# Attention emitted in two halves a pair, inside an attention and two-MoE kernel on one core

## The chip, the cores and the metric

The kernel runs on one NeuronCore of a Trainium2 chip. The metric is the device time of one execution in microseconds, the median of three runs, lower is better. PE is the matrix engine (TensorE), DVE the vector engine, ACT the scalar engine, POOL is GpSimd, and SP issues most DMAs.

## The reference

Three stages follow one another over 4 x 768 = 3072 tokens. Banded attention with sink columns (8 heads of 64, window 128, 4 sinks) gives x; a product of two projections and two more matrices gives x again; a router sends every token to one of 8 experts.

```
keep = is_sink | in_window                       # pos < 4, or 0 <= query - key < 128
scores = where(keep, (q @ k.T) / sqrt(64), -1e9)
a = exp(scores - max);  a = a / (sum(a) + 1e-9)
x = a @ v                                        # then heads side by side: [3072, 512]
x = ((x @ w1) * (x @ w2)) @ w3 @ w_out           # first MoE block, w1 and w2 [512, 1024]
e = argmax(x @ w_gate + modality_bias[modality_id])
out = gate * relu(x @ w1[e]) @ w2[e]             # second MoE block, 8 experts
```

## The kernel before

**Tiles.** The tokens are cut in 12 units of 256 (three to a batch entry, `c` = 0, 1, 2), and the heads in 4 pairs of two. One step through attention is a pair `n` (unit `n // 4`, heads `n % 4`), 48 in all. A unit has two blocks of 128 queries, `j` = 0 and 1. The parts of a pair are these.

- `a_tqk(n)` makes q and k ready with their low parts (by PE for the first 8 pairs, by a transpose on DVE after that).
- `a_scores(n, j)`: 6 matmuls on L458 (three pairs, each for two heads in the two halves of 64 rows of the array) into the one buffer `sp`, then a masking copy (L475) and a maximum (L484) on DVE, two exponentials on ACT (L486), and, deferred, the normalization of `P` on DVE (`norm`, L491 to L497).
- `a_pt(n)` transposes `P` with 4 matmuls (L527); ACT copies the result to `ptf` (L531), and POOL makes two masked copies `ptp` (L536). `a_skT(n)` transposes the sink columns (L509).
- `a_pv(n)` is the product of P and v: 12 matmul instructions on L555 (8 where `c` is 0) with an output of 64 columns of the array for each head, and one for the sinks (L558). ACT and DVE then write the result into `xb` (L561, L566).

**First MoE block.** Units go through `moe1_stream` in 6 groups of two. A group `gr` is a row of pieces, each with a cost: 16 pieces "ab" (12 matmuls on L724, cost 2600), 8 pieces "x2" (6 matmuls on L712, cost 1300), and 8 pieces "late" (6 matmuls on L712, cost 1300) for its second unit. The cost `t` reaches 52,000 with the last "x2" and 62,400 with the last "late". Before the first "late" piece can write, ACT must empty the two `x2p` buffers of the first unit (`route_rows`, L772).

**What sets the order.** `att_stream` is a generator; each `yield` ends a step, and a pair `n` has 5 steps. After every MoE piece `front` calls `att_upto`, which runs attention steps up to a number that grows with `t`: 20 steps evenly over the first 52,000 (so step k of the group follows the first piece whose `t` is over 2600 (k - 1)), then 20 steps over the 8 "late" pieces. A group starts with four steps of its first pair already made. Pairs 9 to 47 lie in the groups 0 to 4; the last group has no attention. Deferred jobs run at the second `tick` after them, and both steps and pieces tick. The framework then puts out each engine's instructions in the order of emission, except that one which its plan finds not ready lets later ones go first. Engines work through their lists in order.

Before the change, the steps of a pair from the second on are: scores of block 0; transposes of pair n - 1; `a_tqk(n + 1)`; scores of block 1; product of pair n - 1.

Of the kernel before, what the change touches and what calls it, by code (L numbers as in the profile page):

```python
# [27 lines left out]
def attention_moe_moe_kernel(ctx, tc, q, k, v, w1, w2, w3, w_out, mod_id, w_gate, mod_bias, e_w1, e_w2, out,  # L28
# [57 lines left out]
    def tick():  # L86
        for fn in waiting[0]:
            fn()
        waiting[0], waiting[1] = waiting[1], []

    def settle():
        while waiting[0] or waiting[1]:
# [253 lines left out]
    def a_load(n):  # L346
        u, p = divmod(n, NP)
        b, c = divmod(u, NC)
        hs = slice(2 * p, 2 * p + 2)
        qk = att.tile([128, 2, UNIT], F32, tag="qk", bufs=2, name="qk")  # L350
        for x, src in enumerate((q, k)):
            if n < BY_PE:
                for j in range(2):
                    s0 = c * UNIT + j * 128
                    nc.sync.dma_start(out=qk[:, x, j * 128:(j + 1) * 128].rearrange("p (h d) -> p h d", h=2),
                                      in_=src[b, hs, s0:s0 + 128, :].rearrange("h s d -> s h d"))
                continue
            for g in range(4):
                h, d0 = 2 * p + g // 2, g % 2 * 32
                nc.sync.dma_start(out=qk[g * 32:(g + 1) * 32, x].rearrange("p (b i) -> p b i", i=32),  # L360
                                  in_=src[b, h, c * UNIT:(c + 1) * UNIT, d0:d0 + 32].rearrange("(b s) i -> s b i", s=32))
        nat[n] = qk

    def a_load_v(n):
        u, p = divmod(n, NP)
        b, c = divmod(u, NC)
        hs = slice(2 * p, 2 * p + 2)
        vn = att.tile([128, 3, 2, D], F32, tag="vn", bufs=3, name="vn")
        for j in range(0 if c else 1, 3):
            s0 = c * UNIT + (j - 1) * 128  # L370
            nc.sync.dma_start(out=vn[:, j], in_=v[b, hs, s0:s0 + 128, :].rearrange("h s d -> s h d"))
        stt["v", n] = vn
        if n and c == 0 and p == 0:
            a_load_sinks(b)
# [143 lines left out]
    def a_pt(n):  # L518
        u, p = divmod(n, NP)
        b, c = divmod(u, NC)  # L520
        P = stt["p", n]
        for j in range(2):
            stt.pop(("norm", n, j))()
        tp = ps_t.tile([128, 4, 128], F32, tag="t", name="pt")
        for j in range(2):
            for h in range(2):
                nc.tensor.transpose(out=tp[:, 2 * j + h, :], in_=P[:, j, h * (KW + NS):h * (KW + NS) + 128], identity=idf)  # L527
        full = att.tile([128, 4, 128], F32, tag="ptf", bufs=1, name="ptf")
        parts = att.tile([128, 2, 2, 2, 128], F32, tag="ptp", bufs=1, name="ptp")
        i0 = 0 if c else 1  # L530
        nc.scalar.activation(out=full[:, 2 * i0:4], in_=tp[:, 2 * i0:4], func=ACTF.Copy)  # L531
        if i0:
            nc.scalar.activation(out=parts[:, 0, 0], in_=tp[:, 0:2], func=ACTF.Copy)
        for a, op in enumerate((ALU.is_ge, ALU.is_gt)):
            sign = 1 - 2 * a
            nc.gpsimd.affine_select(out=parts[:, a, i0:2].rearrange("p j h q -> p (j h) q"), in_=full[:, 2 * i0:4],  # L536
                                    pattern=[[0, 4 - 2 * i0], [sign, 128]], compare_op=op, fill=0.0, base=0,
                                    channel_multiplier=-sign)
        stt["pt", n] = parts
# [34 lines left out]
    def att_stream():  # L574
        a_tqk(0); yield
        a_load(1)
        a_load_sinks(0)
        a_vsink(0)
        yield
        for n in range(NN):  # L580
            if n + 2 < NN:
                a_load(n + 2)
            a_scores(n, 0); yield
            if n:
                a_load_v(n)
                a_pt(n - 1); a_skT(n - 1); yield
            if n + 1 < NN:
                a_tqk(n + 1)
            yield
            a_scores(n, 1); yield  # L590
            if n:
                a_pv(n - 1)
                att_done[0] = n
                if n % (NP * NC) == 0:
                    a_vsink(n // (NP * NC))
            yield
        a_pt(NN - 1); a_skT(NN - 1); yield
        a_pv(NN - 1)
        att_done[0] = NN
        yield  # L600
# [412 lines left out]

    def front():
        att_it = att_stream() if banded else att_stream_full()
        steps = [0]

        def step_att():
            if next(att_it, 0) == 0:
                return False  # L1020
            steps[0] += 1
            tick()
            return True

        def att_upto(target):
            while steps[0] < target and step_att():
                pass

        unit_steps = ATT_STEPS * NP
        begun = 10 if banded else 4  # L1030
        wab_n = W_EARLY
        t = 0.0
        f64_ahead(2)
        if banded:
            a_load(0)
            a_load_v(0)
        f64_ahead(4)
        for i, c in enumerate(startup_stream()):
            t += c
            tick()  # L1040
            if att_done[0] < 2 * NP:
                att_upto(min(0.75 * (i + 1), 8) + 38 * t / 46700)
        early = []
        for gr in range(NU // 2):
            while att_done[0] < (2 * gr + 2) * NP:
                step_att()
            settle()
            last = gr == NU // 2 - 1
            if last:
                for _ in att_it:  # L1050
                    pass
                att_ctx.close()
                pool = p2a.enter_context(tc.tile_pool(name="p2a", bufs=1, side="right", reuse_waits="tile"))
                mem = mem_of(pool, wp, pool, pool, pool, pool, (ps_t, ps_ab, ps_x2, 1))
                p2a_pool.append(pool)
                mem["w1"] = halves(lambda: pool.tile([128, 1024], F32R, tag="w1", bufs=KD, name="w1"), mem["w"])
                rows0 = pool.tile([128, SLOT // 128, ROW], F32, name="xrows")
                t_banks = [mem["pt"], lambda: ps_x.tile([128, 512], F32, tag="x", name="x")]

                def next_bank():  # L1060
                    t_banks.reverse()
                    return t_banks[0]()

                mem["pt"] = next_bank

                def next_early(first=0):
                    slots.append(Slot(SLOT, (NU - 2 if slots else NU - 4) * UNIT, mem))
                    slots[-1].decide(first)

                def first_early():  # L1070
                    next_early(3)
                    slots[0].gather(rows0)

                first_early()
                early = [(10000 + 2000 * i, lambda i=i: slots[0].w1_piece(i)) for i in range(KD)]
                early += [(47000 + 1500 * i, next_early) for i in range(N_EARLY - 1)]
                early += [(57200 + 1300 * i, lambda i=i: slots[0].transposes(i)) for i in range(KD)]
            t, routed, s0 = 0.0, 0, steps[0]
            s1 = begun + (2 * gr + 3) * unit_steps
            for kind, c in moe1_stream(gr):  # L1080
                t += c
                tick()
                while gr == 0 and wab_n < KF and wab_n < W_EARLY + t / 4000:
                    wab_pair(wab_n)
                    wab_n += 1
                    if wab_n == KF:
                        wgate_by_expert()
                        start_ctx.close()
                        sp_[0] = m1_ctx.enter_context(tc.tile_pool(name="m1", bufs=1, reuse_waits="tile"))
                        consts_late()  # L1090
                        load_wgate()
                if last:
                    while early and t >= early[0][0]:
                        early.pop(0)[1]()
                    due = min(t, 46000) / 1100
                else:
                    due = min(t, 46000) / 1100
                while routed < due and kind != "late":
                    routed += 1
                    route_step()  # L1100
                if kind != "late":
                    att_upto(min(s0 + (s1 - s0) * t / 52000, s1))
                else:
                    att_upto(s1 + unit_steps * (t - 52000) / 10400)
            for _, fn in early:
                fn()
        settle()
# [131 lines left out]
```

## Time and profile before

| | |
|---|---|
| runs | 975.64, 975.77, 976.39 us (median 975.77) |
| the profiled execution | 975.55 us, span 973.8 us |
| PE | 932.9 us busy, 96% of the span |
| DVE | 651.8 us busy, 67% |
| ACT | 440.5 us busy, 45% |
| POOL | 167.2 us busy, 17% |

Starts of matmuls are recorded, their ends are modelled and overlap the next start. So a price on PE is best read from the distance between the starts of two rows, and not from the busy time.

### The profile page before, as it was taken

To read this page: it belongs to the slowest core of one execution; us is meant where nothing else is said; L and a number is where in the kernel's file an instruction comes from. 1 tells how busy PE (TensorE), PEld (TensorE's weight loads), DVE (VectorE), ACT (ScalarE), POOL (GpSimd) and SP (SyncE) were. 2 spreads that over 40 slices of the span, in tenths; PEclk is the share of its full clock that TensorE was granted. 3 is DMA by queue.
4 is the path that set the end of the run, shared out by engine and by line. 5 is a ranking of instruction groups with operands and counts; after the bars stand their busy time and mean duration, and the time that the engine had idled before them with its cause. 6 is when DMAs were issued, how large, how long until landed. Compare 5 with 4: busy or idle time off the path is not lost. (4 is left out here: it accounts for less than half of the span.)

```text
span 973.8 us, 15418 instructions
## 1 busy us (share of the span) xinstructions
PE 932.9 (96%) x4840; PEld 709.7 (73%) x4840; DVE 651.8 (67%) x1953; ACT 440.5 (45%) x1218; POOL 167.2 (17%) x253
## 2 busy tenths in 40 slices
PE   4899999999999999999999999999999999999995
PEld 3567677767776777677767776887888888888883
DVE  7956996699659964896599649929934374333422
ACT  3687763454335433553365334314433443344433
POOL 1111121111112111211111112213021214111010
PEclk9999999999999999999999999999999999999998
DMA  8754754123212231236123200512446465443331
GB/s 258 237 149 122 210 121 127 34 53 71 51 23 48 61 56 20 52 71 44 23 53 67 56 9 9 178 40 87 139 164 129 153 69 191 132 149 120 109 134 41
DMA packets 168933, 94.02 MB, mean 97 GB/s; under 512 B 140231, under 2 KB 148679, under 8 KB 168720
## 3 DMA queue, kind: packets, MB, share of 16 engines
q1 hardware_dynamic: 164080, 80.13, 33.6%
q0 software_dynamic: 4768, 12.88, 4.1%
q8 instruction: 39, 0.64, 0.3%
q14 instruction: 46, 0.38, 0.2%
HBM read 80.14 MB, written 13.09 MB: 96 GB/s over the span
## 5 line engine op out<-in xcount | busy, mean ns | idle before, releaser
L724 PE MATMUL ab<-xb,wab 128*128 128x512 f32 x1152 | 288.7, 397 | 1.0 <-DVE g L734 1.0
L724 PEld LDWEIGHTS ab<-xb,wab 128*128 128x128 f32 x1152 | 209.7, 188 | 46.0 <-PE sp L458 1.1
L970 PE MATMUL x<-w 128*128 128x512 f32 x600 | 141.0, 392 | 0.0
L785 DVE CUSTOM_DVE_ANT_0 junk<-rows,wgb 128x512 bf16<-128x512 f32 x192 | 135.7, 707 | 2.0 <-ACT rows L772 0.9
L712 PE MATMUL x2p<-w3o,gh 128*128 128x512 f32 x384 | 128.9, 411 | 0.5 <-ACT gh L701 0.5
L970 PEld LDWEIGHTS x<-w 128*128 128x128 f32 x600 | 111.6, 188 | 23.1 <-DVE w L202 0.4
L536 POOL TENSOR_SCALAR_AFFINE_SELECT ptp<-ptf 128x512 f32<-128x512 f32 (+1 forms) x96 | 66.5, 716 | 308.0 <-ACT ptf L531 308.0
L701 ACT ACTIVATE gh<-g 128x256 fp32r<-128x256 f32 x96 | 39.9, 416 | 119.2 <-DVE g L731 98.6
L486 ACT ACTIVATE P<-sp,st 128x132 f32<-128x132 f32 (+1 forms) x192 | 69.2, 366 | 51.5 <-DVE st L484 45.8
L712 PEld LDWEIGHTS x2p<-w3o,gh 128*128 128x128 f32 x384 | 67.2, 188 | 18.0 <-ACT gh L701 2.9
L202 DVE TENSOR_TENSOR w<-wst,w 128x512 fp32r<-128x512 f32 x112 | 71.4, 685 | 10.5 <-ACT w L201 10.5
L937 DVE SCALAR_TENSOR_TENSOR w<-ab,w 128x512 fp32r<-128x512 f32 x48 | 33.1, 690 | 64.4 <-ACT w L936 64.2
L712 PE MATMUL x2p<-w3o,gl 128*128 128x512 f32 x192 | 76.0, 396 | 0.0
L933 PE MATMUL ab<-w,w 128*128 128x512 f32 x288 | 74.9, 395 | 0.0
L933 PE MATMUL ab<-w 128*128 128x512 f32 x288 | 73.6, 391 | 0.0
L201 ACT ACTIVATE w<-wst 128x512 fp32r<-128x512 f32 x112 | 63.4, 628 | 4.5 <-DMA wst<-in_moe_w_dram 4.5
L458 PE MATMUL sp<-ring,qh 64*128 64x264 f32 (+1 forms) x384 | 61.1, 329 | 3.2 <-ACT P L486 2.2
L458 PEld LDWEIGHTS sp<-ring,qh 64*128 64x128 f32 x384 | 37.0, 185 | 35.8 <-ACT P L486 15.5
L933 PEld LDWEIGHTS ab<-w,w 128*128 128x128 f32 x288 | 53.9, 188 | 12.4
L933 PEld LDWEIGHTS ab<-w 128*128 128x128 f32 x288 | 54.1, 188 | 12.1
L936 ACT ACTIVATE w<-ab 128x512 fp32r<-128x512 f32 x48 | 28.7, 597 | 71.8 <-PE ab L933 71.4
L974 POOL DMA_INDIRECT out_dram<-late,ti x25 | 25.2, 1009 | 203.9 <-ACT late L973 166.6
(201 smaller groups left out, 1392.9 us busy)
## 6 DMA issues: line engine op xcount, KB each, us to landing
wst<-in_moe_w_dram SPq DMA_DIRECT2D x56, 512.0 KB
f64st<-in_moe_w_dram SPq DMA_DIRECT2D x32, 512.0 KB
vn<-in_v_dram SPq DMA_DIRECT2D x128, 64.0 KB
xs<-rows SPq DMA_DIRECT2D x12, 513.0 KB
qk<-in_q_dram SPq DMA_DIRECT2D x160, 32.0 KB
qk<-in_k_dram SPq DMA_DIRECT2D x160, 32.0 KB
f64st<-in_moe_w_out_dram SPq DMA_DIRECT2D x8, 512.0 KB
wgb<-wgt SPq DMA_DIRECT2D x1, 2048.0 KB
```

The lines of the kernel that those rows point to most:

```text
L201: nc.scalar.activation(out=hi, in_=src, func=ACTF.Copy)
L202: lo_eng.tensor_tensor(out=lo, in0=src, in1=f32(hi), op=ALU.subtract)
L458: nc.tensor.matmul(out=sp[:, h, c0:c0 + nk].rearrange("p (a b) -> p a b", b=KW), lhsT=a[hp, j, :], rhs=kr[hp, b_, blocks, c0:c0 + KW], sta ...
L486: nc.scalar.activation(out=rows[:, h], in_=seen[:, h], func=ACTF.Exp, bias=st[:, 0, h:h + 1], accum_out=st[:, 1, h:h + 1])
L536: nc.gpsimd.affine_select(out=parts[:, a, i0:2].rearrange("p j h q -> p (j h) q"), in_=full[:, 2 * i0:4], pattern=[[0, 4 - 2 * i0], [sign, ...
L701: nc.scalar.activation(out=gh, in_=g, func=ACTF.Copy)
L712: nc.tensor.matmul(out=x2p[t], lhsT=a[:, sl], rhs=b_, start=(f == 0 and i == 0), stop=(f == KF - 1 and i == 2))
L724: nc.tensor.matmul(out=bank[nm].rearrange("p (u t) -> p u t", u=2), lhsT=a, rhs=b_, start=(kk == 0 and i == 0), stop=(kk == KD - 1 and i = ...
L785: nc.vector.tensor_tensor_reduce(out=junk, in0=rows[:, t, 0:DM], in1=wgb[0][:, e, :], scale=1.0, scalar=0.0, op0=ALU.mult, op1=ALU.add, ac ...
L933: nc.tensor.matmul(out=hp, lhsT=a[:, fs], rhs=b_, start=(kk == 0 and i == 0), stop=(kk == KD - 1 and i == 2))
L937: nc.vector.scalar_tensor_tensor(out=h[:, 1], in0=hp, scalar=0.0, in1=f32(h[:, 0]), op0=ALU.max, op1=ALU.subtract)
L970: nc.tensor.matmul(out=op, lhsT=a[:, ts], rhs=b_, start=(f == 0 and i == 0), stop=(f == KF - 1 and i == 2))
```

## The change

For pairs with `n > 2 * NP`, that is 9 to 47, the five steps become: (A) the loads, the scores of block 0 and the transposes of pair n - 1; (B) `a_tqk(n + 1)`; (C) the scores of block 1 and the product of pair n - 1; and two empty steps. Nothing is computed otherwise, and no instruction is added or removed. A helper `in_order` would tie PE instructions to their order of emission, but it is used only where `strict[0]` is true, and nothing sets it so.

```diff
         for n in range(NN):
             if n + 2 < NN:
                 a_load(n + 2)
+            if n > 2 * NP:
+                a_load_v(n)
+                a_scores(n, 0)
+                a_pt(n - 1); a_skT(n - 1); yield
+                if n + 1 < NN:
+                    a_tqk(n + 1)
+                yield
+                a_scores(n, 1)
+                a_pv(n - 1)
+                att_done[0] = n
+                if n % (NP * NC) == 0:
+                    a_vsink(n // (NP * NC))
+                yield
+                yield
+                yield
+                continue
             a_scores(n, 0); yield
...
+        strict = [False]
 
         def step_att():
-            if next(att_it, 0) == 0:
+            if (in_order(lambda: next(att_it, 0)) if strict[0] else next(att_it, 0)) == 0:
                 return False
...
-            for kind, c in moe1_stream(gr):
+            strict[0] = False
+            moe_it = moe1_stream(gr)
+            while True:
+                piece = in_order(lambda: next(moe_it, None)) if strict[0] else next(moe_it, None)
+                if piece is None:
+                    break
+                kind, c = piece
```

## Rows read from the trace of the kernel before

**Rows 1.** The page: busy time of the engines over the span.
```profile
PE 932.9 (96%) x4840; PEld 709.7 (73%) x4840; DVE 651.8 (67%) x1953; ACT 440.5 (45%) x1218; POOL 167.2 (17%) x253
```
**Rows 2.** Windows: length, busy us of each engine, granted clock, DMA share, GB/s.
```profile
265.00:289.00 24.00, 24.00 (x132) 18.65 (x131) 11.65 (x38) 9.01 (x26) 4.74 (x8) 1.00 0.13 24
289.00:313.00 24.00, 22.25 (x137) 14.87 (x137) 21.65 (x68) 13.36 (x45) 4.78 (x9) 1.00 0.25 44
```
**Rows 3.** Groups by line on PE, 122 to 610 us (busy, mean, idle before).
```profile
L724 PE MATMUL ab<-xb,wab 128*128 128x512 f32 x973 | 246.8, 398 | 1.0 <-DVE g L734 1.0
...
L458 PE MATMUL sp<-ring,qh 64*128 64x264 f32 (+1 forms) x312 | 48.4, 328 | 2.1 <-ACT P L486 1.8
L555 PE MATMUL xp<-ptp,vn 128*64 128x128 f32 (+1 forms) x432 | 47.3, 323 | 2.9 <-issue 1.7 <-POOL ring L435 0.6 <-POOL ptp L536 0.3
L527 PE MATMUL pt<-idf,P 128*128 128x128 f32 x160 | 27.5, 278 | 4.7 <-DVE P L497 3.3 <-DVE wk L814 1.4
```
**Rows 4.** Timeline of PE, 252.9 to 262 us: start, length, instructions merged.
```profile
253.22 0.39 PE L712 MATMUL x2p<-w3o,gl 128*128 128x512 f32 x1
253.54 0.40 PE L458 MATMUL sp<-ring,qh 64*128 64x264 f32 x2
...
254.10 3.02 PE L724 MATMUL ab<-xb,wab 128*128 128x512 f32 x12
257.05 1.09 PE L555 MATMUL xp<-ptp,vn 128*64 128x256 f32 x12
...
258.29 2.90 PE L724 MATMUL ab<-xb,wab 128*128 128x512 f32 x12
261.13 0.40 PE L458 MATMUL sp<-ring,qh 64*128 64x264 f32 x2
```
**Rows 5.** Timeline of PE at 414 us.
```profile
413.87 0.39 PE L458 MATMUL sp<-ring,qh 64*128 64x264 f32 x2 [0.29 <-ACT P L486]
...
414.44 1.09 PE L555 MATMUL xp<-ptp,vn 128*64 128x256 f32 x12
```
**Rows 6.** Timeline of PE, 263 to 270 us.
```profile
263.17 2.89 PE L724 MATMUL ab<-xb,wab 128*128 128x512 f32 x12
265.90 0.60 PE L527 MATMUL pt<-idf,P 128*128 128x128 f32 x4
...
266.47 3.01 PE L724 MATMUL ab<-xb,wab 128*128 128x512 f32 x12
269.32 0.62 PE L712 MATMUL x2p<-w3o,gh 128*128 128x512 f32 x2
```
**Rows 7.** Timeline of PE, 389 to 395 us.
```profile
389.48 0.40 PE L712 MATMUL x2p<-w3o,gl 128*128 128x512 f32 x1
389.80 0.65 PE L555 MATMUL xp<-ptp,vn 128*64 128x256 f32 x2
390.38 0.74 PE L712 MATMUL x2p<-w3o,gh 128*128 128x512 f32 x2
...
391.29 0.86 PE L555 MATMUL xp<-ptp,vn 128*64 128x256 f32 x8
392.08 0.73 PE L712 MATMUL x2p<-w3o,gh 128*128 128x512 f32 x2
...
392.98 0.43 PE L555 MATMUL xp<-ptp,vn 128*64 128x128 f32 x2
...
393.65 0.39 PE L458 MATMUL sp<-ring,qh 64*128 64x264 f32 x2
...
394.22 0.66 PE L527 MATMUL pt<-idf,P 128*128 128x128 f32 x4
```
**Rows 8.** Timeline of ACT over the same stretch.
```profile
389.21 0.60 ACT L772 ACTIVATE rows<-x2p 128x512 f32<-128x512 f32 x1 [0.47 <-PE x2p L712]
...
390.71 0.61 ACT L772 ACTIVATE rows<-x2p 128x512 f32<-128x512 f32 x1
```
**Rows 9.** Timeline of PE at 407 us.
```profile
406.76 1.09 PE L555 MATMUL xp<-ptp,vn 128*64 128x256 f32 x12 [0.64 <-issue]
```

More of the change, by code (lines that the diff above doesn't have):

```diff
@@ L89, in tick, with in_order @@
         waiting[0], waiting[1] = waiting[1], []
+    issued = [None]
+    def in_order(fn):
+        traced = nc.cur_bb.bb.instructions
+        first = len(traced)
+        got = fn()
+        for ins in traced[first:]:
+            if ins.engine == mybir.EngineType.PE:
+                if issued[0] is not None:
+                    tc.add_manual_dep(ins, issued[0], mybir.DependencyInfo(mybir.DependencyClass.NoSync,
+                                                                           mybir.DependencyReason.DATA), reason="in order")
+                issued[0] = ins.name
+        return got
     def settle():
```

## The prediction, as it was made

> **What bounds the kernel now.** I read the page first: PE is busy for 96% of the span and no other engine for more than 73%, the weight loads of PE itself included [rows 1]. So PE's list sets the time, and a change can win only by making what PE does cheaper or by taking away waits on it. The groups by line, over the stretch in which the changed pairs run, bound the second: before scores, product and transposes PE sat idle for 2.1 + 2.9 + 4.7 = 9.7 us in all [rows 3]. The windows say where. In a regular stretch of a group PE has no gap at all and DVE works for 11.65 of 24 us; in the stretch that starts with the "late" pieces DVE works for 21.65 of 24 us and PE has 1.75 us without work [rows 2]. So there are two kinds of place: a regular one, where PE alone decides and its order follows the emission, and a crowded one (some 45 us a group, from the late pieces to the first fifth of the next group), where attention runs as its results come in and MoE fills the holes. The clock is 1.00 of full speed, the 2.4 GHz level, in both [rows 2]. What is left is the price of PE's order, and the timeline has it.
>
> **Prices of a change of kind.** A row of MoE matmuls runs at 0.2275 us each: twelve take from 263.17 to 265.90, 2.73 us, and the transposes that follow cost no extra to enter [rows 6]. Into scores there is an entry price: 253.22 to 253.54 is 0.32, so 0.09 more than 0.23 [rows 4]. Twelve MoE matmuls between scores and a product take from 254.10 to 257.05, 2.95 us, 0.22 over 2.73: 0.09 is the entry to the product and 0.13 an exit price behind the scores. Twelve between a product and scores take 2.84 (258.29 to 261.13): entry 0.09, and behind a product next to no exit, 0.02 [rows 4]. Behind transposes twelve take 2.85 (266.47 to 269.32), so these have an exit of 0.12 of their own [rows 6].
>
> **The change, part by part.** No instruction is added or removed, and the order in which attention puts out its PE work stays the same (scores 0, transposes, scores 1, product). Only the MoE pieces between them move.
>
> *Scores of block 1 next to the product (C).* What stood on both sides of the MoE row, exit 0.13 and entry 0.09, goes, if scores then run into the product for no more than they run into MoE. Six scores matmuls to MoE take 0.56 (253.54 to 254.10) [rows 4]; the one case in which a product follows directly takes 0.57 (413.87 to 414.44) [rows 5]. So a C saves 0.22 - 0.01 = 0.21 us. How many: the steps C are the 4th, 9th, 14th and 19th of a group, and the product before was the 6th, 11th, 16th and 21st. The 4th falls in the crowded stretch, so I count three a group and four in the first group, which has little in front of it: 16 for five groups, 3.4 us. Both ends: all 39 pairs give 8.2 us, none 0. I take 16, since only in the regular stretch does the order on PE follow the emission.
>
> *Scores of block 0 next to the transposes (A).* The scores' exit of 0.13 goes. Scores to transposes takes 0.57 (393.65 to 394.22), against 0.56, and the four transposes behind them last 0.66 [rows 7] against 0.60 [rows 6]. So 0.13 - 0.01 - 0.06 = 0.06, times 16: 1.0 us. Ends: 0 and 39 x 0.06 = 2.3.
>
> *The junction to the late pieces.* The product that was step 21, first behind the first late piece, becomes part of step 19 and leaves this place. Here PE must wait for ACT to empty the two buffers (0.60 us each, at 389.21 and 390.71) [rows 8], and the product is what fills the hole, torn in three parts by MoE threes. From 389.80 to 393.65 are 3.85 us; without six MoE matmuls (1.37) and the entry of the scores (0.09) that is 2.39 [rows 7], against 1.24 for a whole product (257.05 to 258.29) [rows 4]: 1.15 lost. The five groups have such a place at 194.16, 290.31, 389.80, 487.28 and 583.44 us, three torn in three and two in two parts; for two I take half, so 3 x 1.15 + 2 x 0.58 = 4.6 us. What fills the hole now is A: transposes, which enter free, and scores, which may be cut up to twice at 0.22 each (entry and exit), 5 x 0.44 = 2.2. I take 4.6 - 2.2 = 2.4; ends 0 (something is torn as dearly) and 4.6.
>
> *What I cost at nothing.* The loads of v are put out one step sooner on SP's queue, behind the same loads of q and k; v(n) is read only a pair later, which covers it. The empty steps only let deferred jobs run. ACT and DVE get scores and transposes, or scores and product, in one bunch; in the regular stretch DVE's 12 free us of 24 [rows 2] cover that, and the banks that it must empty for MoE have the next x2 or ab piece (6 or 12 x 0.2275) in front of their next use. If that cover went, PE would stand before L724, which idled 1.0 us in all this stretch [rows 3]. Waits of PE in the crowded stretch I leave as they are; they can change by up to the 9.7 us that exist [rows 3], either way. `strict[0]` is never true, so the helper costs nothing.
>
> *Sum.* 3.4 + 1.0 + 2.4 = 6.8 us off the profiled execution of 975.55: 968.75. The median of the runs is 0.22 above that execution, so about 969.0.
>
> A rule that speaks against C: the Trainium skill, TensorE: Matmul & The Clock Gate, Part 3, says that a weight load runs under a matmul in flight only when the two use different row groups. Scores use halves of the rows and the product all, so by it the first weight load of a product (64 columns, 53 ns by the formula of that page's section on LDWEIGHTS, an estimate) would stand open in each C; 16 of these are 0.85 us and the sum would be 5.9. The row at 414.44 does not show it, so my sum leaves it out.
>
> **Rivals.**
> 1. *The junction stays as dear* (chance 0.15). The plan tears whatever stands there: a cut scores group, or the product of the step 19 pushed back to the hole. For it: the hole itself remains, since ACT's two copies remain [rows 8]. Against it: transposes are in reach and enter free. Time: 975.77 - 4.4 = 971.4.
> 2. *Next to each other is worth nothing* (0.15). The only uninterrupted case of C is a single row, and it stands behind a wait [rows 5]; if scores ran into the product 0.2 us later than into MoE, as they would if a weight load that the last MoE matmul hid stood open, or if the plan finds the product not ready and puts MoE between, C saves nothing. With the junction unchanged too, 975.77 - 1 = 974.8, down to no change.
> 3. *The product waits for POOL* (0.20; the other side). Between a pair's transposes and its product in the late stretch stand one MoE piece and the scores where there were two pieces and the scores: 6 x 0.2275 = 1.37 us less for ACT, POOL's two masked copies and DVE's low part of the sinks. One product there already waits 0.64 us [rows 9]. There are 4 such pairs a group, 20 in all. If all wait 0.64, that is 12.8 - 6.8 = 6.0 us slower, 981.8; it decides from 6.8 / 0.64 = 11 waits on, and 14 give 977.9. Behind the waiting product on PE's list is everything, MoE too. Against it: products that the plan finds late are passed by MoE matmuls, and in the crowded stretch the order of attention itself does not change.
>
> **How the numbers follow.** Forecast 0.50, with its own range 965.5 to 971.4 (the junction between 0 and 4.6, waits changed by 1 or 2 us); rivals 0.15, 0.15 and 0.20. A measurement of this kernel can tell 0.2%, about 1.95 us, from no change, so 973.8 and 977.7 are the bounds. Faster: 0.50 + 0.15 = 0.65; within: 0.15; slower: 0.20. To hold eight in ten the range takes the forecast and the first two rivals whole and the foot of the third: 965.5 to 977.
>
> **What would show it.** In the timeline of a regular stretch scores are followed within 0.57 us by a product or by transposes, and the twelve MoE matmuls behind take 2.73 to 2.85 us, not 2.95. Around the late pieces the product is in one part, 1.24 us. The idle time before L458, L555 and L527 stays near 9.7 us, and that before L724 near 1.0. The first late piece comes some 1.3 us a group earlier than before, added up group by group. Wrong would be: MoE matmuls between scores and product in the regular stretch (rival 2), torn scores at the junction with the same total (rival 1), or idle time before L555 of more than 7 us (rival 3).

## The result, and the profile after

The changed kernel takes 965.06 us (median of 964.83, 964.92, 965.20 and 965.63) against 975.87 for the kernel before, run on the same chip: a ratio of 0.9889, 95% interval 0.9872 to 0.9907, 10.8 us faster. The forecast was 969.0, 6.8 us faster. The sign was right, and each of the three places that the prediction named did gain; 4 us were missing, and the time lies 0.44 us below the range.

Line numbers move: L724 is now L755, L712 is L743, L458 is L473, L555 is L570, L527 is L542, L772 is L803. So do the copies and sums around them: DVE's normalization of `P`, L497, is L512, ACT's exponentials, L486, are L501, POOL's masked copies, L536, are L551, and DVE's subtraction that makes the low part of the sinks, L514, is L529.

The page of the kernel after, busy time by engine, answers to [rows 1]. PE has the same 4840 matmuls and is still busy for 96% of a span of 963.0 us.

```profile
PE 924.0 (96%) x4840; PEld 711.2 (74%) x4840; DVE 649.3 (67%) x1953; ACT 440.2 (46%) x1218; POOL 168.2 (17%) x253
```

The timeline of PE in a regular stretch of the kernel after (start, length, merged instructions; it answers to [rows 4, 5, 6]). Scores at 250.87 run into a product at 251.44, 0.57 us later, and scores at 259.59 into transposes at 260.16, 0.57 us later. Behind the product, six MoE matmuls take 252.68 to 254.06, 1.38 us, which is 6 at 0.2275 and next to nothing, and 24 more take 5.53, which is 24 at 0.2275 and 0.07 for the entry to scores: nothing is left of the exit price that stood behind scores.

```profile
250.87 0.39 PE L473 MATMUL sp<-ring,qh 64*128 64x264 f32 x2
...
251.44 1.09 PE L570 MATMUL xp<-ptp,vn 128*64 128x256 f32 x12
...
252.68 0.63 PE L743 MATMUL x2p<-w3o,gh 128*128 128x512 f32 x2
...
254.06 5.60 PE L755 MATMUL ab<-xb,wab 128*128 128x512 f32 x24
259.59 0.40 PE L473 MATMUL sp<-ring,qh 64*128 64x264 f32 x2
...
260.16 0.66 PE L542 MATMUL pt<-idf,P 128*128 128x128 f32 x4
```

The junction to the late pieces, PE of the kernel after (answers to [rows 7]). The product is whole, 285.36 to 286.60, 1.24 us. A single matmul of the next scores fills the hole in front of the first late piece (0.32 us, 289.41 to 289.73), then six MoE matmuls go in one row, and the other five scores follow. The scores are torn, as I had feared, once and not twice. But the one cut is dear: 0.32 us for the single matmul, and the six MoE matmuls behind it take 1.59 us to the next scores instead of 1.37, while the five scores that are left take 0.56, as long as six. That is 0.54 us.

```profile
284.79 0.39 PE L473 MATMUL sp<-ring,qh 64*128 64x264 f32 x2
...
285.36 1.09 PE L570 MATMUL xp<-ptp,vn 128*64 128x256 f32 x12
...
286.60 0.62 PE L743 MATMUL x2p<-w3o,gh 128*128 128x512 f32 x2
...
289.41 0.39 PE L473 MATMUL sp<-ring,qh 64*128 64x264 f32 x1
289.73 0.73 PE L743 MATMUL x2p<-w3o,gh 128*128 128x512 f32 x2
...
291.32 0.39 PE L473 MATMUL sp<-ring,qh 64*128 64x264 f32 x1
...
291.88 0.66 PE L542 MATMUL pt<-idf,P 128*128 128x128 f32 x4
```

ACT over the same stretch (answers to [rows 8]). The two copies that empty the buffers start 0.84 us apart, not 1.50, since no exponentials of the last scores lie between them any more.

```profile
288.84 0.60 ACT L803 ACTIVATE rows<-x2p 128x512 f32<-128x512 f32 x1 [0.43 <-PE x2p L743]
...
289.68 0.58 ACT L803 ACTIVATE rows<-x2p 128x512 f32<-128x512 f32 x1
```

The waits of PE in the kernel after, 122 to 610 us (total, times, longest; they answer to the idle times of [rows 3]). Scores and transposes wait less, products more; MoE waits no longer in this stretch.

```profile
PE pt L542 <- DVE P L512: 2.6, 5, 0.9
PE xp L570 <- POOL ptp L551: 1.8, 5, 0.6
PE xp L570 <- POOL wgst L789: 1.3, 1, 1.3
PE sp L473 <- ACT P L501: 0.8, 4, 0.3
PE xp L570 <- issue: 0.7, 2, 0.4
PE pt L542 <- DVE wk L845: 0.6, 1, 0.6
```

The rows of products need care, for a wait is put down to the engine that the profile saw last, and that one had often long been done. The longest wait of a product names a POOL constant (L789). Here are POOL, DVE and PE around it:

```profile
129.51 3.83 POOL L551 TENSOR_SCALAR_AFFINE_SELECT ptp<-ptf 128x512 f32<-128x512 f32 x2 [11.22 <-ACT ptf L546]
133.28 0.51 POOL L789 MEMSET wgst<- 32x512 f32 x1
...
133.86 0.41 DVE L529 TENSOR_TENSOR pskT<-xp,pskT 8x256 fp32r<-8x256 f32 x1
...
134.37 1.09 PE L570 MATMUL xp<-ptp,vn 128*64 128x256 f32 x12 [1.33 <-POOL wgst L789]
```

The constant is done 0.57 us before the product starts. DVE's low part of the sinks is done at 134.27, 0.10 before. It reads the sinks from the tile `xp` that the product then writes, so the product has to come behind it. Five of the eight product waits over 0.15 us in this kernel, 3.1 of the 4.2 us, end 0.10 us after L529 did and 0.47 to 1.24 us after the masked copies did. Where POOL's copy is last, as at 400.05, the product starts 0.05 us behind it. So most of what products wait for is DVE's L529.

**Where the time came from.** All of it lies between the first L724 matmul (122.09 us, after: 122.34) and the last product (609.44, after: 598.88): 487.35 against 476.54 us. What is left of the two profiled executions is nearly the same, 975.55 - 487.35 = 488.20 and 964.83 - 476.54 = 488.29. In that distance PE idles for 10.62 us before and 8.37 after. So 8.56 us are price of PE's order and 2.25 us are waiting.

I cut the five groups at the same matmuls: "start" is the first 60 ab matmuls, "regular" runs from the 61st to the 181st, "junction" from there to the seventh late one, "late" to the next group's first. "Over" is length, less idle, less the content at undisturbed prices (a MoE matmul 0.2275, six scores 0.76, a product 1.02 and 0.32 for its sinks, a transpose 0.11, a matmul of the router's ranks 0.03), summed over the groups. It allows for work that crossed a border. The prices of scores and products are set too high: undisturbed they take 0.56 and 1.24 [rows 4]. So an "over" can be negative, and only differences between kernels count.

| stretch | before: length, idle, over | after | junction pair only | three other pairs only |
|---|---|---|---|---|
| start | 117.30, 3.23, 1.51 | 120.01, 3.50, 1.52 | 119.72, 3.42, 1.63 | 115.94, 2.77, 0.60 |
| regular | 217.82, 1.39, 1.00 | 213.29, 0.62, -2.44 | 218.32, 1.93, 0.96 | 213.11, 0.14, -2.46 |
| junction | 55.20, 0.00, 5.03 | 51.78, 0.00, 0.95 | 51.80, 0.00, 0.97 | 55.20, 0.00, 5.04 |
| late | 92.64, 5.69, 4.11 | 86.87, 3.93, 2.85 | 86.14, 3.90, 2.15 | 92.66, 5.73, 4.09 |

The last two columns are experiments, told below. Regular: 3.44 us of price. Junction: 4.08 us of price. Late: 1.26 of price and 1.76 of waiting, in a stretch that I had left as it is. One scores group and one product moved from late to start; with 0.56 and 1.24 for them late is 1.56 cheaper and start 0.31 dearer, and the sum is the same.

### The profile page after: what moved, and what is told of

The parts are those of the page before. It is cut to its first block, busy times and chain, and to the rows that moved or that the text cites. A ratio compares the mean times of both kernels' runs of the same rounds, so it can differ in the third digit from the quotient of the medians.

```text
span 963.0 us, 15420 instructions
## 1 busy us (share of the span) xinstructions
PE 924.0 (96%) x4840; PEld 711.2 (74%) x4840; DVE 649.3 (67%) x1953; ACT 440.2 (46%) x1218; POOL 168.2 (17%) x253
## 5 line engine op out<-in xcount | busy, mean ns | idle before, releaser
L755 PE MATMUL ab<-xb,wab 128*128 128x512 f32 x1152 | 281.2, 394 | 0.0
L755 PEld LDWEIGHTS ab<-xb,wab 128*128 128x128 f32 x1152 | 212.6, 188 | 44.6 <-ACT xb L576 0.2
L743 PE MATMUL x2p<-w3o,gh 128*128 128x512 f32 x384 | 128.0, 407 | 0.5 <-ACT gh L732 0.5
L551 POOL TENSOR_SCALAR_AFFINE_SELECT ptp<-ptf 128x512 f32<-128x512 f32 (+1 forms) x96 | 66.4, 715 | 335.8 <-ACT ptf L546 335.8
L501 ACT ACTIVATE P<-sp,st 128x132 f32<-128x132 f32 (+1 forms) x192 | 68.9, 365 | 25.8 <-DVE st L499 24.1
L743 PEld LDWEIGHTS x2p<-w3o,gh 128*128 128x128 f32 x384 | 67.5, 189 | 13.8 <-ACT gh L732 1.1
L743 PE MATMUL x2p<-w3o,gl 128*128 128x512 f32 x192 | 76.2, 397 | 0.0
L762 DVE TENSOR_TENSOR g<-ab,bs 128x256 f32<-128x256 f32 x48 | 20.2, 420 | 80.1 <-PE ab L755 55.1
L473 PE MATMUL sp<-ring,qh 64*128 64x264 f32 (+1 forms) x384 | 63.1, 329 | 1.9 <-ACT P L501 1.0
L473 PEld LDWEIGHTS sp<-ring,qh 64*128 64x128 f32 x384 | 38.2, 185 | 35.9 <-issue 15.4
```

The source lines that it names most:

```text
L473: nc.tensor.matmul(out=sp[:, h, c0:c0 + nk].rearrange("p (a b) -> p a b", b=KW), lhsT=a[hp, j, :], rhs=kr[hp, b_, blocks, c0:c0 + KW], sta ...
L501: nc.scalar.activation(out=rows[:, h], in_=seen[:, h], func=ACTF.Exp, bias=st[:, 0, h:h + 1], accum_out=st[:, 1, h:h + 1])
L743: nc.tensor.matmul(out=x2p[t], lhsT=a[:, sl], rhs=b_, start=(f == 0 and i == 0), stop=(f == KF - 1 and i == 2))
L755: nc.tensor.matmul(out=bank[nm].rearrange("p (u t) -> p u t", u=2), lhsT=a, rhs=b_, start=(kk == 0 and i == 0), stop=(kk == KD - 1 and i = ...
```

## The experiments

Each was timed beside the kernel before on the same chip: 975.98 us for A only, C only, C taken apart and product back; 975.64 for four pairs, the two with the table later and all pairs; 975.67 for the other three. "Places" are counted in the listed order of PE from the first MoE matmul on: how often scores run into a product, into transposes, how often something cuts a product (a MoE row in 8 of the 12 cases before, scores in 4), and torn scores. Distance is that from the first ab matmul to the last product, its sinks included, in the one execution that was profiled, which can differ from the median by up to 1 us.

| kernel | median us, ratio (95%) | into product, transposes, cuts, torn | distance, idle, the rest |
|---|---|---|---|
| before | 975.87 | 7, 9, 12, 0 | 487.35, 10.62, 476.73 |
| whole change | 965.06, 0.9889 (0.9872 to 0.9907) | 29, 26, 4, 5 | 476.54, 8.37, 468.17 |
| A only | 972.63, 0.9967 (0.9955 to 0.9980) | 8, 29, 12, 0 | 484.13, 9.19, 474.94 |
| C only | 970.55, 0.9947 (0.9933 to 0.9961) | 30, 8, 3, 5 | 481.73, 13.22, 468.51 |
| C taken apart | 969.65, 0.9935 (0.9922 to 0.9949) | 10, 26, 4, 5 | 481.06, 8.28, 472.78 |
| product back | 971.57, 0.9953 (0.9939 to 0.9967) | 21, 29, 9, 0 | 483.27, 11.80, 471.47 |
| junction pair only | 969.10, 0.9929 (0.9916 to 0.9941) | 8, 14, 0, 5 | 480.59, 9.57, 471.02 |
| three other pairs only | 970.17, 0.9947 (0.9933 to 0.9960) | 21, 23, 12, 0 | 481.31, 8.96, 472.35 |
| four pairs | 964.60, 0.9887 (0.9872 to 0.9903) | 22, 26, 0, 5 | 476.11, 9.09, 467.02 |
| transposes first | 967.85, 0.9926 (0.9913 to 0.9939) | 30, 18, 3, 0 | 479.09, 12.31, 466.78 |
| C only, table later | 969.35, 0.9933 (0.9919 to 0.9946) | 30, 8, 3, 5 | 480.34, 11.66, 468.68 |
| whole, table later | 964.93, 0.9892 (0.9877 to 0.9907) | 29, 26, 4, 5 | 476.51, 8.29, 468.22 |
| all pairs | 967.09, 0.9910 (0.9895 to 0.9925) | 30, 26, 4, 5 | 477.23, 8.80, 468.43 |

The theory was that the gain is the price of PE's order: so much for each place. The rivals were that attention standing earlier makes PE wait less, and that only the junction counts.

**C taken apart.** The product goes to the step behind the scores, so that a MoE piece comes between.

```diff
                 a_scores(n, 1)
+                yield
                 a_pv(n - 1)
...
                 yield
                 yield
-                yield
```

> The whole change with C taken apart again: scores of block 1 in the third step, the product in the fourth, a MoE piece between, and one empty step. Product still ahead of the late pieces. Listed order: 10 scores into product, 26 scores into transposes, no cut of a product, 5 torn scores. Theory 1: 0.6 + 1.0 + 8 x 0.54 - 1.1 = 4.8 us below before, 971.1, so 6 us (nineteen places and some) slower than the whole change less what idle time does: 4 us by 19 x 0.21, 969.1, where idle time stays as in the whole change. Theory 2: as the whole change, 965 to 966. Theory 3: as the whole change, 965 to 966.

Measured 969.65. The first theory gave 971.1, and 969.1 where idle time stays as in the whole change; the other two gave 965 to 966. This is the cleanest pair: idle is the same (8.28 and 8.37), transposes, cuts and torn scores are the same, and 19 fewer places where scores run into a product cost 472.78 - 468.17 = 4.61 us, 0.24 each, against the 0.21 that I had read from two rows.

**C only.**

```diff
                 a_scores(n, 0)
-                a_pt(n - 1); a_skT(n - 1); yield
+                yield
+                a_pt(n - 1); a_skT(n - 1)
+                yield
...
                 yield
                 yield
-                yield
```

> Only C: scores of block 1 next to the product, in the fourth step; scores of block 0 and the transposes stay in steps of their own. Listed order of PE: 30 places where scores run into a product (7 before, 29 in the whole change), 8 where scores run into transposes (9 and 26), no torn product (8 cuts before), 5 torn scores. Theory 1, prices of entering and leaving on PE (0.21 us a place of the first kind, 0.06 of the second, about 0.54 a cut of a product, 0.22 a cut of scores): 23 x 0.21 + 8 x 0.54 - 5 x 0.22 = 8.0 us below before, 967.9. Theory 2, the gain comes from transposes and scores standing one step earlier, so that PE waits less: at most half of the gain, 970 to 973. Theory 3, only the whole product at the late pieces counts: 966 to 968.

Measured 970.55. The rest, 468.51, is 8.22 us below before, as the prices have it (8.0), but PE idles 2.60 us more, 13.22. So the time lies in the range of the second theory (970 to 973) and not at the first theory's 967.9, but not for the second theory's reason: PE waits more, not less. The waiting is in the regular stretch (5.42 us, against 1.39 before and 0.62 in the whole change), and the timeline of POOL shows it. The router's two table writes (L851) stand between the two masked copies (L551) of one pair's transposes; the second copy starts at 253.78 instead of right behind the first.

```profile
250.34 0.64 POOL L551 TENSOR_SCALAR_AFFINE_SELECT ptp<-ptf 128x512 f32<-128x512 f32 x1 [16.32 <-ACT ptf L546]
251.30 1.20 POOL L851 DMA_INDIRECT tab<-tokid,ix  x1 [0.32 <-DVE sm L834]
252.79 0.98 POOL L851 DMA_INDIRECT tab<-tokid,ix  x1 [0.30 <-issue]
253.78 0.65 POOL L551 TENSOR_SCALAR_AFFINE_SELECT ptp<-ptf 128x512 f32<-128x512 f32 x1
```

On PE of the same kernel the product waits for that copy, with all the MoE behind it:

```profile
254.48 1.09 PE L570 MATMUL xp<-ptp,vn 128*64 128x256 f32 x12 [1.13 <-POOL ptp L551]
```

The like happens at 448.2 and 543.8 us (1.64 and 1.01). In all three the product starts 0.05 us after the second copy ended, so here the wait is POOL's. In the listed order of POOL, neither the kernel before nor the whole change has a table write between two copies of a pair.

**A only.**

```diff
                 a_pt(n - 1); a_skT(n - 1); yield
+                yield
...
                 a_scores(n, 1)
+                yield
                 a_pv(n - 1)
...
                 yield
-                yield
-                yield
```

> Only A: scores of block 0 next to the transposes, one step earlier; scores of block 1 and the product in the steps of before. Listed order: 8 scores into product, 29 scores into transposes, 8 cuts of products as before. Theory 1: 1 x 0.21 + 20 x 0.06 = 1.4 us below before, 974.5. Theory 2: half of the gain, 969 to 972. Theory 3: no change, 975.9.

Measured 972.63, 3.35 us faster, more than twice what the prices give. The rest is 1.79 lower, somewhat more than they have it (1.4): 0.08 a place and not 0.06. The other 1.43 us are idle time. A wait of MoE for DVE of 0.96 us at the head of the first group is gone, here and in the whole change; in its place a product waits 0.69 for POOL here, and 1.33 for DVE in the whole change. One wait of transposes for the router's ranks, which use the same PSUM buffer, is 0.84 shorter: 1.39 us before, 0.55 here, 0.62 after. So the time falls between the first theory (974.5) and the second (969 to 972), and the second holds for 1.43 of these 3.35 us.

**The product back behind the first late piece**, for one pair of a group.

```diff
+            if n > 2 * NP and n % (2 * NP) == NP + 1:
+                ...
+                a_scores(n, 1)
+                yield
+                yield
+                a_pv(n - 1)
```

> The whole change, but for the one pair of a group whose product stood behind the first late piece before: its product goes back there (fifth step). Listed order: 21 scores into product, 29 scores into transposes, 5 cuts of products, scores whole. Theory 1: 14 x 0.21 + 20 x 0.06 + 3 x 0.54 = 5.7 us below before, 970.2. Theory 2: 965 to 966, since four of five pairs are as in the whole change. Theory 3: all of the gain but a little is lost, 973 to 975.

Measured 971.57, 6.5 us slower than the whole change: 3.30 of price and 3.43 of waiting. That is 1.4 us above the first theory and below the third's 973 to 975. One pair in eight carries more than half of the gain. Its late stretch is about as dear as before in price (over 4.29) and in idle (5.30 us). That accounts for 1.37 of the 3.43 of waiting; 1.46 lie in the start stretches. The profiled execution, 972.52, is the slowest of the five, so the waiting may be put too high.

**The junction pair only, and the three pairs ahead of it only.**

```diff
-            if n > 2 * NP:
+            if n > 2 * NP and n % 8 in (5,):
```

```diff
-            if n > 2 * NP:
+            if n > 2 * NP and n % 8 in (2, 3, 4):
```

> The change for one pair of a group alone (n mod 8 = 5), the one whose product stood behind the first late piece. Listed order of PE: 8 scores into product and 14 into transposes (7 and 9 before), all 12 cuts of products of before gone, 5 torn scores; one masked copy on POOL torn by table writes in one group. Theory of prices: 0.24 + 5 x 0.08 + 12 x 0.5 - 5 x 0.22 = 5.5 us below before, less about 1 us of waiting for POOL, 971.1 against 975.6. My prediction's term for the junction, 2.4, and little else: 973.0. Rival, the product is not dearer in parts: 975.

> The change for the three pairs of a group ahead of that one (n mod 8 = 2, 3, 4). Listed order of PE: 21 scores into product, 23 into transposes, all 12 cuts of products as before. Theory of prices: 14 x 0.24 + 14 x 0.08 = 4.5 us below before, 971.1, and up to 2 us less where the waits of the whole change come with it. Rival, most of the gain is at the junction: 974.

Measured 969.10 and 970.17: 6.6 and 5.5 us faster. The table of stretches separates them. The three other pairs change the regular stretch by as much as the whole change does (over -2.46 and -2.44) and leave junction and late as they were (5.04 and 4.09). The junction pair alone leaves the regular stretch (0.96) and changes the junction by as much as the whole change does (0.97 and 0.95), and with it the late stretch: 1.96 us of price and 1.79 of waiting. So what I had left out follows from that one pair. The two sums of waiting are made up differently, though: late, before, scores wait 1.56, transposes 2.25 and products 1.86 us; with the junction pair only 1.65, 1.43 and 0.83, in the whole change 0.52, 1.32 and 2.09. Only the transposes wait less in both. All 12 cuts of products are gone in it, also the four that scores made later in the crowded stretch. The expected 971.1 of the junction pair had 1 us more waiting in it, and 1.05 less came; the three other pairs came within 1 us of their 971.1.

**Four pairs of a group**, with the late ones as before.

```diff
-            if n > 2 * NP:
+            if n > 2 * NP and n % 8 in (2, 3, 4, 5):
```

> The whole change only for the four pairs of a group whose steps lie in its first 20 steps (n mod 8 = 2, 3, 4, 5); the four in the late pieces as before. Listed order of PE: 22 scores into product, 26 scores into transposes, no cut of a product, 5 torn scores; POOL's masked copies untouched by table writes. Theory of prices plus the waits of the whole change: 15 x 0.24 + 17 x 0.08 + 2.2 + 2.2 = 9.4 us below before, 966.6. Rival, the late stretch, where PE waits, gives half of the gain: 969 to 971.

Measured 964.60; its interval and that of the whole change overlap. It is 2.0 us below what I expected, and far from the rival's 969 to 971. The four late pairs of a group, half of the changed ones, bring nothing that can be told from noise. It is the fastest median here, too close to the whole change to call it faster.

**Transposes first at the hole.** The four pairs, and for the next pair the transposes ahead of the scores.

```diff
+            if n > 2 * NP and n % (2 * NP) == 6:
+                a_load_v(n)
+                a_pt(n - 1); a_skT(n - 1); yield
+                a_scores(n, 0); yield
+                a_tqk(n + 1); yield
+                a_scores(n, 1); yield
+                a_pv(n - 1)
```

> The change for the four pairs of a group's first 20 steps, and for the pair behind the first late piece (n mod 8 = 6) the transposes put out ahead of its scores, so that what fills the hole at ACT's two copies is transposes. Listed order of PE: 30 scores into product, 18 scores into transposes, 3 cuts of products (none in the run of four pairs), no torn scores (5 in it and in the whole change). Theory of prices: 8 x 0.24 - 8 x 0.08 + 5 x 0.22 - 3 x 0.5 = 0.9 us below the run of four pairs, 963.7; below the whole change by 1.3. Rival, the hole stays and something else is paid for it: 964.5 to 966.

Measured 967.85, slower than the four pairs and above both expectations. The order of PE is cheaper by less than counted, 0.24 and not 0.9 (the rest 466.78 against 467.02), though the junction falls to 0.10 over. And scores one step later leave attention behind: PE idles 12.31 us, 7.08 of it in the start stretches (4.16 with four pairs), mostly products. Here are the two rows of its waits that the profile puts down to POOL and to nothing that it shows:

```profile
PE xp L570 <- POOL ptp L551: 3.6, 6, 0.9
...
PE xp L570 <- issue: 1.8, 4, 0.6
```

The five longest are 0.59, 0.59, 0.79, 0.78 and 0.94 us. But POOL is not what they wait for. At 426.39 the copies were done 0.83 us before, and DVE's L529 0.10 before, held up by a normalization ahead of it on DVE's list:

```profile
423.89 1.67 POOL L551 TENSOR_SCALAR_AFFINE_SELECT ptp<-ptf 128x512 f32<-128x512 f32 x2 [6.65 <-ACT ptf L546]
...
425.00 0.85 DVE L512 TENSOR_TENSOR P<-P,st 128x264 f32<-128x264 f32 x1
425.87 0.41 DVE L529 TENSOR_TENSOR pskT<-xp,pskT 8x256 fp32r<-8x256 f32 x1
...
426.39 0.87 PE L570 MATMUL xp<-ptp,vn 128*64 128x256 f32 x8 [0.79 <-POOL ptp L551]
```

Nine of the ten product waits over 0.15 us in this kernel, 5.1 of 5.8 us, end 0.10 us after L529 did and 0.44 us or more after the copies did. This is the prediction's third rival in another kernel, too little time between a pair's transposes and its product, but with DVE as the engine that comes last.

**The router's table writes one step later**, in C only and, as a control, in the whole change.

```diff
         nc.vector.tensor_copy(out=ix, in_=s2)
+        yield
```

> C only, as in the first experiment, but the router writes its two table entries by POOL one of its steps later. The listed order of PE has the same number of places of every kind; on POOL the pair of table writes no longer stands between the two masked copies of one pair's transposes, where it stood in 3 of 5 groups (at 254.5, 448.2 and 543.8 us the product waited 1.13, 1.64 and 1.01 us). Theory, the missing gain of C only is the product behind POOL's table writes: 3.8 us less than C only, 966.8. Rival, these waits come from the product standing close behind its transposes and only move: 970 to 971.

> The whole change with the router's table writes one of its steps later, the control to the C-only run with the same shift. No masked copy is torn in either, the listed order of PE has the same counts. Theory: no change against the whole change, 964.8 to 965.6. Rival, the later table write helps by itself: 963 or less.

The control gives 964.93, no change. C only gives 969.35 (five runs from 967.55 to 970.95), 1.2 us less and not 3.8, between theory and rival; its interval and that of C only overlap, so even the 1.2 are not clear of noise. The three waits are gone in the profiled execution, but two others have come, 1.79 and 0.85 us. Ahead of both DVE waits for the load of k, 5.89 and 5.18 us, so that the transposes and what follows them are late. The first product starts 0.10 us after DVE's L529 ended, the second 0.05 after POOL's copy:

```profile
366.20 0.71 DVE L422 STREAM_TRANSPOSE qk<-qk 128x512 f32<-128x512 f32 x1 [5.89 <-DMA qk<-in_k_dram]
```
```profile
369.22 0.87 PE L570 MATMUL xp<-ptp,vn 128*64 128x256 f32 x8 [1.79 <-POOL ptp L551]
```

And the load was issued late, since SP's in-order queue stood for 8.7 us until the router's row store before it had landed (the waits of SP's queue, 320 to 372 us):

```profile
SPq L375 <- DMA xs<-rows: 8.7, 1, 8.7
```

So POOL's table writes are the cause of the three waits that they were named for; how much of the missing gain of C only they are isn't shown. Why the store landed so late there stays open.

**All pairs**, so also 1 to 8 in the startup stretch.

```diff
-            if n > 2 * NP:
+            if n > 0:
```

> The whole change from the first pairs on (n > 0), so also for pairs 1 to 8 in the startup stretch. If PE sets the time there too, 8 more places of each kind: up to 8 x 0.3 = 2.4 us below the whole change, 962.7. If other engines and the loads set the startup, as DVE before the startup matmuls does for 8 us: no change, 964.5 to 966. If the two halves make the products of these pairs, which wait for ACT in their middle, dearer: 966 to 968.

Measured 967.09, within the third expectation, but its interval and that of the whole change overlap, and one of its four runs is 965.06. The first MoE matmul comes at 123.74 us, 1.40 later than in the whole change; in the kernels that leave the startup alone it comes anywhere from 121.84 to 123.60, so this alone shows little. Behind it 0.69 is lost: one wait of MoE for DVE of 1.52 us has come, and products wait 1.4 less. No gain from the startup pairs is shown, and no sure loss.

## Why the prediction was right in kind and wrong in size

**What bounds it.** Right: PE stays at 96%, no instruction changed, and 8.56 of 10.8 us are the price of its order.

**C and A.** Right. I took 3.4 + 1.0 = 4.4 us for 16 pairs; without the junction pair, 15 pairs at the measured rest give 476.73 - 472.35 = 4.38. That the sums are so close is in part luck: the prices are 0.24 and 0.08 and not 0.21 and 0.06, for one pair less. What I called the one case of scores running into a product was one of seven in the trace, all at 0.56 or 0.57 us. The listed order has 22 more C places and not 16, since the crowded stretch has some too; those bring little, as the run of four pairs shows (15 more, and no slower). Rival 2, that standing next to each other is worth nothing, falls by the run with C taken apart. The Trainium skill, TensorE: Matmul & The Clock Gate, Part 3, would have a weight load stand open between scores and product; 0.57 us at 250.87 against 0.56 from scores to MoE [rows 4] shows no such load. That comparison alone doesn't settle it, since by the same rule a load would stand open from scores to MoE too; but MoE matmuls, which all use the whole array, start every 0.2275 us in a row with a weight load of 0.188 us each (the page of the kernel after), so loads do run under matmuls of the same rows here, and the trace disagrees with the rule. The Trainium skill, TensorEngine Tiling (Array Packing), Key Properties, says that a change of tiling mode drains the engine; the 0.24 us that a C place saves agree with one such change less, but leaving a product costs only 0.02 [rows 4] and leaving transposes, in the full mode, 0.12 [rows 6], so that draining is the price is not shown.

**The junction.** The mechanism was right: ACT's two copies make a hole, the product fell into it in parts, and now it stands whole. The term was somewhat small: 4.08 us of price, of which 1.32 are the five C places there that the term above had counted (over 2.27 in C taken apart, 0.95 in the whole change), so 2.8 against 2.4. Its two parts were both too small. A product in two parts loses 0.86 us and not the 0.58 that I took by halving: 194.16 to 197.44 is 3.28, less 1.37, 0.09 and the 0.96 of a whole product of this kind. With 1.14 for three parts the torn products cost 5.1 and not 4.6. The torn scores cost 0.54 us a cut in three groups and 0.48 in two, 2.6 and not 2.2. The difference is 2.5; the 0.3 us that are left I can't place. Rival 1 falls.

**The step that failed: "Waits of PE in the crowded stretch I leave as they are".** And with them I left its prices, for the reason that the order of attention there does not change. It does not, but its start does: the junction pair's product is done before the late pieces and no longer in their way. The late stretch then runs 1.26 us cheaper, where I had nothing, and waits 1.76 less, 3.0 of the 4.0 us missing. That this follows from the junction pair is shown by the runs with that pair only and without it (over 2.15 and 4.09, idle 3.90 and 5.73), and by the run with its product put back (4.29 and 5.30). Transposes wait less for DVE's normalization in both the kernel with that pair only and the whole change; by which link the rest of the waiting fell, whether DVE's list or the buffers of `sp` and `xp`, stays open. The last 1.0 us is 0.4 at the junction, 0.4 of C and A (3.44 + 1.32 against 4.4) and 0.5 us less idle time in the start and regular stretches together, 4.62 before and 4.12 after, less 0.2 lost behind the fifth group.

**The other side.** Rival 3 did not come in the whole change: PE stands idle before products for 4.2 us, 1.3 more than before, and the one wait of 1.33 in the first group is as much. It named the wrong engine, too: the wait of 0.64 us that gave it its price [rows 9] ends 1.25 us after POOL's copies did and 0.10 us after DVE's low part of the sinks, which it named only beside POOL. It is no empty threat: C only pays 2.6 us more waiting than before, transposes first 1.7. The range went wrong with the failing step. Its low end had the junction at its best, 4.6, and some 1.3 us less waiting; the junction gave 2.8 and the waiting 2.25, and the late stretch's 1.26 of price had no place in it. Of the signs named, idle time before the three lines came to 8.4 and not 9.7, and the first late piece did not come earlier group by group: from the first ab matmul it came at 72.64 us before and at 72.97 after in the first group, and the gain begins with the second.

## What to carry to other kernels

Where PE is full, price its order by the distance between starts: a group of scores between MoE matmuls cost 0.09 to enter and 0.13 to leave, a product cut in three 1.14, scores cut once 0.54, and putting two such groups side by side saved 0.24 a time. The place worth most is where PE has a hole that something must fill, here one pair in eight. A cheaper order is given back if a step comes nearer to a slower engine's result, so look on the lists of DVE, POOL and SP for what will stand ahead of it. And hold a wait's named engine against its end time: where it ended long before the wait did, look for an engine that ended just before.

## What the runs showed of the hardware that was not expected

Two indirect table writes of 128 rows hold POOL from 251.30 to 253.78, 2.48 us, and a masked copy that was ready waits behind them. A single scores matmul in front of MoE costs 0.32 us (289.41 to 289.73), more than half of the 0.56 for all six, and the five that follow later take 0.56 again (291.32 to 291.88). A product starts 0.10 us after the end of DVE's L529 where that is last and 0.05 us after POOL's masked copy where that is last (134.37 and 400.05 us in the kernel after). A product of 12 instructions and its sinks take 1.24 us whole; cut in 2, 8 and 2 with the sinks they take 0.58, 0.79 and 0.68 us, 2.05, without the MoE between them (290.31 to 294.14 in the kernel before).
